# A fused recurrence and two-layer kernel: the first layer cut into seven tiles, one in float32 and six split, instead of two and five

## The chip, the cores and the metric

The kernel runs on one core of a Trainium2 chip. The metric is the device time of one execution in microseconds; the figure that counts is the median of the runs.

## The reference, cut to what matters

For each of 4 batches and 8 heads a state of 48 x 48 is carried over 768 positions; the output of a position is read from the state and from the position's own outer product, then the state is decayed by w and the outer product is added. The result, as 3072 tokens of 384, goes through two layers without any residual: the first is `h = max(x @ w_in, 0)`, then `h * h @ w_out` (384 to 2048 to 384); the second is `(x @ w_a) * (x @ w_b) @ w_out` (384 to 1536 to 384).

```python
for t in range(S):
    cur = einsum('bhd,bhe->bhde', u * k[t], v[t])
    y[t] = einsum('bhd,bhde->bhe', r[t], state + cur)
    state = w[t][..., None] * state + einsum('bhd,bhe->bhde', k[t], v[t])
x = y as (3072, 384)
x = maximum(x @ w_in, 0) ** 2 @ w_out
out = ((x @ w_a) * (x @ w_b)) @ w_out2
```

## The kernel before

**Units.** The recurrence is done in chunks of 128 positions. A unit is one batch and one chunk; there are 24, in the order chunk by chunk, four batches in each (`units`), so that unit i is batch i % 4 of chunk i // 4. A unit goes through `prepare` (two scans and some seven more DVE instructions, a ScalarE pass and eight ScalarE scalings of the identity), `scores` (PE, L238 and L242; two predicated copies on DVE, L246), `mix` (PE, L260, L266, L273; the state update on DVE, L291 and L293) and, for all but the first four, `split_x` (L305 on ScalarE, L306 on DVE), which writes the unit's 128 columns of x as a pair of fp32r numbers, high and low part. `prepare` also issues the loads of the unit two further on (`load_unit`, on SyncE's queue); lkr, the tile of k and r, has two buffers.

**First layer.** It is done in tiles of tokens. In each tile 16 steps f run over the hidden dimension. A step makes hp, 128 hidden rows for all tokens of the tile (9 or 3 matmuls), then t = relu(hp) * hp (ScalarE, then DVE), and two steps later `x2_step` adds the product with w_out to three accumulators. hp has two PSUM buffers. The units of the *next* tile are worked on between the steps: `bursts` puts scores and mix of a unit at given steps (BURSTS: eight steps for four units).

Two kinds of tiles exist. The units 0 to 3 (chunk 0) are done in two float32 tiles of 256 columns (loop `half_n`, L401): three plain float32 matmuls for hp (L417) and three for the accumulators (L410). The units 4 to 23 are done in five tiles of 512 columns (loop over c, L442) in split form: `mm3` makes each product of three fp32r matmuls (L310, L311, L312: high by high, high by low, low by high), and t is split as well (`split_g`: gh on ScalarE, L370, gl on DVE, L371).

**Weights.** The 32 blocks of w_in and w_out come as raw 64-bit data. `decode_w1` loads and decodes them into float32 (two instructions each on ScalarE, L41 and L43, and on DVE, L42 and L44), two blocks in each step of the first float32 tile. `split_w1` makes the fp32r pair of a block (L144 on ScalarE, L145 on DVE): four stand in the last steps of the second float32 tile, the others in the first split tile, two a step. The 36 blocks of the second layer's weights are decoded from the second split tile on (`narrow_load`, `narrow_store`), written to DRAM as float32, and in the last tile of the first layer read back (`load_w2`, L160, three buffers ws) and split (`split_w2`, L167 on ScalarE and L168 on DVE), two in a step.

**Order.** The code above is only a priority order: the scheduler of the framework puts the instructions of each engine in an order of its own, by its model of the times, and moves work forward where buffers allow it. The engines then run strictly in that order.

**Second layer.** Six tiles of 512 tokens in split form: bp and ap (9 matmuls of 512 columns each), their product, its split, and 12 matmuls of 384 columns in `o_step` (L519 to L521).

Of the kernel before, what the change touches and what calls it, by code (L numbers as in the profile page):

```python
# [20 lines left out]
C = 128  # L21
NC = S // C
units = [(b, c) for c in range(NC) for b in range(B)]
NU = len(units)
# [47 lines left out]
def chunked_path(ctx, tc, flags, krT, wT, krn, vn, u, w1, w2, w3, w4, w5, out):  # L72
# [59 lines left out]
    def decode_w1():  # L132
        load_w1(3)
        if raw_q:
            dst, n, raw = raw_q.pop(0)
            f = dst[n] = wp.tile([128, 384], F32, tag="w", name="wf")
            decode(nc, f, raw, near)
            split_q.append((dst, n, f))
# [45 lines left out]
        loaded[i] = w, kr, v, nn  # L184

    xt = {}
    x0 = {}
    unit = {}

# [62 lines left out]
    def mix(i):  # L252

        b, c = units[i]
        st = unit.pop(i)
        A, v, s = st["A"], st["v"], states[b]
        ps = p_at.tile([128, G, C], F32, tag="at", name="py")
        if c > 0:
            for g in range(G):
                pe.matmul(  # L260
                    out=ps[0:GP, g, :], lhsT=s[:, g].rearrange("p j d -> p (j d)")[:, 0:GP],
                    rhs=st["r"][:, g, :], start=(g == 0), stop=False, skip_group_check=True,
                )
        for g in range(G):
            for j in range(2):
                pe.matmul(  # L266
                    out=ps[64 * j:64 * j + D, g, :], lhsT=v[:, 2 * g + j, :], rhs=A[:, j, g, :],
                    start=(c == 0), stop=True, skip_group_check=True,
                )
        if c < NC - 1:  # L270
            pk = p_at.tile([128, G, 2, D], F32, tag="at", name="pk")
            for g in range(G):
                pe.matmul(out=pk[0:GP, g], lhsT=st["kt"][:, g, :], rhs=v[:, 2 * g:2 * g + 2, :], start=True, stop=True)  # L273

        def post():
            if c > 0:
                x = at.tile([128, G, C], F32, tag="x", name="xf", bufs=2)
            else:
                if b % 2 == 0:
                    x0[b // 2] = xp.tile([128, G, 2, C], F32, tag="x", name="x0")  # L280
                x = x0[b // 2][:, :, b % 2, :]
# [14 lines left out]
            return (lambda: split_x(i, x)) if c > 0 else None  # L296
        return post

    def split_x(i, xf):
        b, c = units[i]  # L300
        if c not in xt:
            xt[c] = xp.tile([128, 2, 3, T], F32R, tag="x", name="x")
        o = slice(b * C, (b + 1) * C)
        hi, lo = xt[c][:, 0, :, o], xt[c][:, 1, :, o]
        act.activation(out=hi, in_=xf[:, 0:3], func=AF.Copy)  # L305
        dve.tensor_tensor(out=lo, in0=xf[:, 0:3], in1=hi.bitcast(F32), op=ALU.subtract)  # L306

# [59 lines left out]
    def split_g(t):  # L367
        gh = gp.tile([128, T], F32R, tag="gh", name="gh")
        gl = gp.tile([128, T], F32R, tag="gl", name="gl")
        act.activation(out=gh, in_=t, func=AF.Copy)  # L370
        dve.tensor_tensor(out=gl, in0=t, in1=gh.bitcast(F32), op=ALU.subtract)  # L371
        return gh, gl


    def bursts(units_of, at_steps):

        return {f: (units_of[n // 2], n % 2) for n, f in enumerate(at_steps)}

    def burst(plan, f):
        if f not in plan:  # L380
            return None
        i, second = plan[f]
        return (mix if second else scores)(i)
# [14 lines left out]
            act.dma_start(out=x2d[:, m, tok0:tok0 + n], in_=e)  # L398


    for half_n in range(2):  # L401
        x = x0.pop(half_n)
        N = 2 * C
        acc = [p_acc.tile([128, N], F32, tag="acc", name="acc") for _ in range(3)]
        gg = {}

        def x2_step(f):
            t = gg.pop(f)
            for m in range(3):
                pe.matmul(out=acc[m], lhsT=w_out[f][:, m * 128:(m + 1) * 128], rhs=t, start=f == 0, stop=f == 15)  # L410

        plan = bursts((2, 3), (1, 5, 8, 12)) if half_n == 0 else bursts((4, 5, 6, 7), BURSTS)
        prepare(2 if half_n == 0 else 4)
        for f in range(16):
            hp = p_mm.tile([128, N], F32, tag="mm", name="hp")
            for k in range(3):
                pe.matmul(  # L417
                    out=hp, lhsT=w_in[f][:, k * 128:(k + 1) * 128],
                    rhs=x[:, k].rearrange("p b t -> p (b t)"), start=k == 0, stop=k == 2,
                )  # L420
            post = burst(plan, f)
            t = gg[f] = gp.tile([128, N], F32, tag="gh", name="g")
            act.activation(out=t, in_=hp, func=AF.Relu)
            dve.tensor_tensor(out=t, in0=t, in1=hp, op=ALU.mult)
            if half_n == 0:
                decode_w1()
            if tails:
                tails.pop(0)()
            after(plan, f, post)
            if f >= 2:  # L430
                x2_step(f - 2)
            if half_n == 0:
                decode_w1()
            elif f >= 12:
                split_w1()
        x2_step(14)
        x2_step(15)
        while tails:
            tails.pop(0)()
        store_acc(acc, half_n * N, N)  # L440

    narrow_n = [0]  # L442
    for c in range(1, NC):
        x = xt.pop(c)
        xh, xl = x[:, 0], x[:, 1]
        last = c == NC - 1
        acc = [p_acc.tile([128, T], F32, tag="acc", name="acc") for _ in range(3)]
        gg = {}

        def x2_step(f):  # L450
            gh, gl = gg.pop(f)
            for m in range(3):
                mm3(acc[m], w_out[f], m, gh, gl, f == 0, f == 15)

        plan = {} if last else bursts(range(4 * c + 4, 4 * c + 8), BURSTS)
        if not last:
            prepare(4 * c + 4)
        for f in range(16):
            hp = p_mm.tile([128, T], F32, tag="mm", name="hp")
# [3 lines left out]
            t = gp.tile([128, T], F32, tag="t", name="t", bufs=2)  # L463
            act.activation(out=t, in_=hp, func=AF.Relu)  # L464
            dve.tensor_tensor(out=t, in0=t, in1=hp, op=ALU.mult)  # L465
            gg[f] = split_g(t)
            if c == 1:
                split_w1()
            if tails:
                tails.pop(0)()  # L470
            after(plan, f, post)
            if f >= 2:
                x2_step(f - 2)
            if c == 1:
                split_w1()
            elif (c - 2) * 16 + f >= narrow_n[0] * 1.2:
                narrow_n[0] += 1
                narrow_load()
            if narrow_q and (len(narrow_q) > 1 or not narrow):
                narrow_store()  # L480
            if last:
                if f >= 1:
                    load_w2()
                    load_w2()
                if f >= 3:
                    split_w2()
# [9 lines left out]
        store_acc(acc, c * T, T)  # L496
        if c + 1 == NC - 1:
            while narrow_q:
                narrow_store()

# [8 lines left out]
    for i in range(NC):  # L509
# [13 lines left out]
        for f in range(12):  # L523
# [14 lines left out]
            gg[f] = split_g(bs)  # L538
            if i == 0:
                split_w2()  # L540
            if f >= 2:
# [187 lines left out]
```

## Time and profile before

| what | value |
|---|---|
| runs | 1047.23 us median of 3 (1043.69 to 1050.37) |
| profiled execution, its own time | 1045.72 us |
| span of the profiled execution, first to last instruction | 1044.0 us |
| PE busy | 996.7 us, 95% |
| DVE busy | 535.7 us, 51% |
| ACT busy | 443.2 us, 42% |
| mean granted TensorE clock | 0.990 |

PE is TensorE's matmuls, PEld its weight loads, DVE VectorE, ACT ScalarE, SP SyncE. A busy time is the union of the records of an engine in a stretch. The records of neighbouring matmuls overlap, so what a matmul takes from its engine is read from the distance of two starts, not from its duration. One float32 matmul of 256 columns leaves two records, an fp32r one leaves one. The first 118 us hold the start and the first float32 tile, the stretch up to about 174 us the second; the first split tile runs to about 277 us, the last one from about 518 to 592 us; then comes the second layer.

### The profile page before, as it was taken

How to read it: one execution, taken by the hardware profiler on the slowest of the kernel's cores; microseconds unless marked ns; L12 is line 12 of the kernel's file. 1: busy time of each engine (PE TensorE's matmuls, PEld its weight loads, DVE VectorE, ACT ScalarE, POOL GpSimd, SP SyncE). 2: the span in 40 equal slices, each digit the busy share in tenths (PEclk: the TensorE clock that was granted, in tenths of full speed). 3: DMA queues.
4: the chain of work that ended last, by engine and by line, in shares of the span. 5: the costliest groups of instructions: out<-in, count | busy, mean ns of one | idle time of the engine just before them, and what ended most of it. 6: DMA issues, size and time to landing. Idle time of an engine off the chain costs nothing. (4 is left out here: it accounts for less than half of the span.)

```text
span 1044.0 us, 13596 instructions
## 1 busy us (share of the span) xinstructions
PE 996.7 (95%) x5154; PEld 841.7 (81%) x5154; DVE 535.7 (51%) x890; ACT 443.2 (42%) x912; POOL 67.8 (6%) x60
## 2 busy tenths in 40 slices
PE   3789999998899999999999999999999999999996
PEld 2578888776688888888888888888888888888885
DVE  8999787888887568464355522222222222221221
ACT  5687456676754454354255521312312312212221
POOL 4232001000111001000000000000000000000000
PEclk9999999998899999999999999999999999999999
DMA  9776116766741222111133300100100100100000
GB/s 267 221 251 208 51 52 199 229 222 226 253 139 58 82 70 70 37 58 42 43 116 93 112 1 1 61 1 1 61 1 1 41 1 2 40 1 31 1 1 33
DMA packets 47019, 88.14 MB, mean 84 GB/s; under 512 B 7008, under 2 KB 25568, under 8 KB 46944
## 3 DMA queue, kind: packets, MB, share of 16 engines
q1 hardware_dynamic: 40464, 77.74, 24.0%
q10 hardware_dynamic: 6480, 9.44, 2.5%
q8 instruction: 42, 0.69, 0.3%
q14 instruction: 33, 0.27, 0.1%
HBM read 69.46 MB, written 16.52 MB: 82 GB/s over the span
## 5 line engine op out<-in xcount | busy, mean ns | idle before, releaser
L537 DVE TENSOR_TENSOR t<-ap,t 128x512 f32<-128x512 f32 x72 | 49.8, 692 | 283.9 <-PE ap L312 283.8
L370 ACT ACTIVATE gh<-t 128x512 fp32r<-128x512 f32 x152 | 95.9, 631 | 187.0 <-DVE t L537 132.4
L371 DVE TENSOR_TENSOR gl<-t,gh 128x512 fp32r<-128x512 f32 x152 | 107.5, 707 | 66.8 <-ACT gh L370 66.5
L528 ACT ACTIVATE t<-bp 128x512 f32<-128x512 f32 x72 | 43.0, 597 | 163.0 <-PE bp L312 163.0
L310 PE MATMUL hp<-x,w 128*128 128x512 f32 x240 | 96.4, 402 | 8.1 <-DVE t L465 8.0
L519 PE MATMUL acc<-w,gh 128*128 128x384 f32 x288 | 96.9, 336 | 0.0
L520 PE MATMUL acc<-w,gh 128*128 128x384 f32 x288 | 96.7, 336 | 0.0
L311 PE MATMUL acc<-gl,w 128*128 128x512 f32 x240 | 94.4, 393 | 1.9 <-DVE gl L371 1.8
L521 PE MATMUL acc<-w,gl 128*128 128x384 f32 x288 | 95.1, 337 | 0.0
L312 PE MATMUL hp<-x,w 128*128 128x512 f32 x240 | 95.0, 396 | 0.0
L311 PE MATMUL hp<-x,w 128*128 128x512 f32 x240 | 95.0, 396 | 0.0
L465 DVE TENSOR_TENSOR t<-t,hp 128x512 f32<-128x512 f32 x80 | 54.5, 681 | 77.5 <-ACT t L464 77.5
L312 PE MATMUL acc<-gh,w 128*128 128x512 f32 x240 | 93.9, 391 | 0.0
L310 PE MATMUL acc<-gh,w 128*128 128x512 f32 x240 | 93.6, 408 | 0.0
L312 PE MATMUL bp<-x,w 128*128 128x512 f32 x216 | 85.2, 395 | 0.0
L311 PE MATMUL bp<-x,w 128*128 128x512 f32 x216 | 85.1, 394 | 0.0
L464 ACT ACTIVATE t<-hp 128x512 f32<-128x512 f32 x80 | 47.3, 591 | 88.3 <-PE hp L312 88.2
L312 PE MATMUL ap<-x,w 128*128 128x512 f32 x216 | 84.1, 389 | 0.0
L311 PE MATMUL ap<-x,w 128*128 128x512 f32 x216 | 84.1, 389 | 0.0
L310 PE MATMUL ap<-x,w 128*128 128x512 f32 x216 | 84.0, 389 | 0.0
L310 PE MATMUL bp<-x,w 128*128 128x512 f32 x216 | 84.0, 389 | 0.0
L225 ACT ACTIVATE A<-ident,dd 128x128 f32<-128x128 f32 x192 | 58.7, 391 | 8.7 <-DVE dd L222 8.2
(93 smaller groups left out, 1753.0 us busy)
## 6 DMA issues: line engine op xcount, KB each, us to landing
raw<-in_w SPq DMA_DIRECT2D x68, 384.0 KB, 5.3
lkr<-in_krT SPq DMA_DIRECT2D x24, 448.0 KB, 4.0
nn<-in_krn SPq DMA_DIRECT2D x24, 384.0 KB, 4.1
w2d<-f SPq DMA_DIRECT2D x36, 192.0 KB, 3.6
ws<-w2d SPq DMA_DIRECT2D x36, 192.0 KB, 2.3
lw<-in_wT SPq DMA_DIRECT2D x24, 226.2 KB, 3.1
vn<-in_vn SPq DMA_DIRECT2D x24, 192.0 KB, 2.7
out<-e ACTq DMA_DIRECT2D x24, 192.0 KB, 1.9
```

Of the source, the lines that this page charges most:

```text
L225: act.activation(out=A[:, h % 2, h // 2, :], in_=ident, func=AF.Copy, scale=dd[:, h])
L310: pe.matmul(out=out, lhsT=wt[:, 0, sl], rhs=rhs_hi, start=first, stop=False)
L311: pe.matmul(out=out, lhsT=wt[:, 0, sl], rhs=rhs_lo, start=False, stop=False)
L312: pe.matmul(out=out, lhsT=wt[:, 1, sl], rhs=rhs_hi, start=False, stop=last)
L370: act.activation(out=gh, in_=t, func=AF.Copy)
L371: dve.tensor_tensor(out=gl, in0=t, in1=gh.bitcast(F32), op=ALU.subtract)
L464: act.activation(out=t, in_=hp, func=AF.Relu)
L465: dve.tensor_tensor(out=t, in0=t, in1=hp, op=ALU.mult)
L519: pe.matmul(out=acc[t], lhsT=ph[:, sl], rhs=w_o[f][:, 0, :], start=(f == 0), stop=False)
L520: pe.matmul(out=acc[t], lhsT=ph[:, sl], rhs=w_o[f][:, 1, :], start=False, stop=False)
L521: pe.matmul(out=acc[t], lhsT=pl[:, sl], rhs=w_o[f][:, 0, :], start=False, stop=(f == 11))
L537: dve.tensor_tensor(out=bs, in0=ap, in1=bs, op=ALU.mult)
```

## The change

The tiles of the first layer are cut in another way. A list `tiles` names their units: the first has units 0 and 1, then come five of four units (2 to 5, 6 to 9, ... 18 to 21), and the last has units 22 and 23. Only the first one is float32; the second float32 tile is gone. The last tile is split and has 256 columns. So 16 steps of three and three float32 matmuls of 256 columns go, and 16 steps of nine and nine fp32r matmuls of 256 columns come, at the other end of the layer. The units that are worked on in the float32 tile are now 2 to 5 (before 2 and 3, and 4 to 7 in the second one); the last full tile has only two units to work on. Units 2 and 3 are written in split form now. `split_w1` starts in the last four steps of the only float32 tile. `narrow_load` is spaced by 1.6 steps, where it was 1.2.

```diff
+    tiles = [(0, 1)] + [tuple(range(i, i + 4)) for i in range(2, NU - 2, 4)] + [(NU - 2, NU - 1)]
...
-            if c > 0:
+            if i > 1:
                 x = at.tile([128, G, C], F32, tag="x", name="xf", bufs=2)
...
-            return (lambda: split_x(i, x)) if c > 0 else None
+            return (lambda: split_x(i, x)) if i > 1 else None
...
     def split_x(i, xf):
-        b, c = units[i]
-        if c not in xt:
-            xt[c] = xp.tile([128, 2, 3, T], F32R, tag="x", name="x")
-        o = slice(b * C, (b + 1) * C)
-        hi, lo = xt[c][:, 0, :, o], xt[c][:, 1, :, o]
+        n, o = (i + 2) // 4, (i + 2) % 4
+        if n not in xt:
+            xt[n] = xp.tile([128, 2, 3, T], F32R, tag="x", name="x")
+        o = slice(o * C, (o + 1) * C)
+        hi, lo = xt[n][:, 0, :, o], xt[n][:, 1, :, o]
...
-    for half_n in range(2):
-        x = x0.pop(half_n)
-        N = 2 * C
...
-        plan = bursts((2, 3), (1, 5, 8, 12)) if half_n == 0 else bursts((4, 5, 6, 7), BURSTS)
-        prepare(2 if half_n == 0 else 4)
...
+    plan = bursts(tiles[1], BURSTS)
+    prepare(2)
+    for f in range(16):
+        hp = p_mm.tile([128, N], F32, tag="mm", name="hp")
...
+        decode_w1()
+        if f >= 12:
+            split_w1()
...
-    for c in range(1, NC):
-        x = xt.pop(c)
-        xh, xl = x[:, 0], x[:, 1]
-        last = c == NC - 1
-        acc = [p_acc.tile([128, T], F32, tag="acc", name="acc") for _ in range(3)]
+    for n in range(1, len(tiles)):
+        x = xt.pop(n)
+        N = len(tiles[n]) * C
+        xh, xl = x[:, 0, :, 0:N], x[:, 1, :, 0:N]
+        last = n == len(tiles) - 1
...
-        plan = {} if last else bursts(range(4 * c + 4, 4 * c + 8), BURSTS)
+        plan = {} if last else bursts(tiles[n + 1], BURSTS)
...
-            if c == 1:
+            if n == 1:
                 split_w1()
...
-            elif (c - 2) * 16 + f >= narrow_n[0] * 1.2:
+            elif (n - 2) * 16 + f >= narrow_n[0] * 1.6:
                 narrow_n[0] += 1
                 narrow_load()
```

In the excerpts of the order below the lines of the changed kernel are one higher than before as far as L372 (the float32 steps keep theirs, L410 to L424), and one lower at L464, where t is multiplied by hp.

The first place is DVE where most of the first layer's weights are split. Before, it lies in the second float32 tile; g is the product of a float32 step, w a split weight block, lkr a unit's tile of k and r in `prepare`:

```order
L424 TENSOR_TENSOR g_1087<-g_1087,hp_1065 128x256
L145 TENSOR_TENSOR w_1683<-wf_552,w_1683 128x384
L205 TENSOR_TENSOR lkr_1126<-lkr_1126,fq_1390 112x512
L207 TENSOR_TENSOR lkr_1126<-lkr_1126,fq_1390 112x512
L145 TENSOR_TENSOR w_1695<-wf_604,w_1695 128x384
L209 SCALAR_TENSOR_TENSOR lkr_1126<-lw_1125,lkr_1126 112x512
L424 TENSOR_TENSOR g_1155<-g_1155,hp_1136 128x256
L145 TENSOR_TENSOR w_1733<-wf_618,w_1733 128x384
L145 TENSOR_TENSOR w_1788<-wf_628,w_1788 128x384
```

In the changed kernel it comes after the last g of the only float32 tile, three splits behind it, and the excerpt ends with t_1116, the first product of the first split tile:

```order
L247 COPY_PREDICATED A_1220<-mask_132,ps_1294 128x512
L247 COPY_PREDICATED A_1220<-mask_132,ps_1295 128x512
L201 RECIPROCAL d2_135<-fq_1416 112x4
L206 TENSOR_TENSOR lkr_1084<-lkr_1084,fq_1416 112x512
L214 TENSOR_TENSOR pe2_1424<-fq_1416,half_136 112x8
L145 TENSOR_TENSOR w_1281<-wf_559,w_1281 128x384
L145 TENSOR_TENSOR w_1316<-wf_588,w_1316 128x384
L145 TENSOR_TENSOR w_1332<-wf_602,w_1332 128x384
L145 TENSOR_TENSOR w_1352<-wf_616,w_1352 128x384
L202 SCALAR_TENSOR_TENSOR fq_1416<-lw_1083,d2_135 112x516
L464 TENSOR_TENSOR t_1116<-t_1116,hp_1091 128x512
```

Before, two splits stand between two float32 products; now seven splits, two predicated copies and part of a `prepare` stand between the last float32 product and the first split one.

The second place is DVE in the last tile of the first layer; ws is a block of the second layer's weights read back from DRAM, w its split, t and gl the two products of a step. Before:

```order
L465 TENSOR_TENSOR t_5091<-t_5091,hp_5081 128x512
L168 TENSOR_TENSOR w_5255<-ws_5179,w_5255 128x384
L371 TENSOR_TENSOR gl_5095<-t_5091,gh_5094 128x512
L168 TENSOR_TENSOR w_5258<-ws_5181,w_5258 128x384
L465 TENSOR_TENSOR t_5127<-t_5127,hp_5117 128x512
```

and in the changed kernel:

```order
L464 TENSOR_TENSOR t_5389<-t_5389,hp_5379 128x256
L168 TENSOR_TENSOR w_5588<-ws_5477,w_5588 128x384
L372 TENSOR_TENSOR gl_5393<-t_5389,gh_5392 128x256
L168 TENSOR_TENSOR w_5591<-ws_5479,w_5591 128x384
L464 TENSOR_TENSOR t_5425<-t_5425,hp_5415 128x256
```

The pattern of a step is the same, two splits in each, but the step's own two products have half the columns, as have its 18 matmuls.

## Rows read from the trace of the kernel before

**Rows 1.** The page's first part, busy time of each engine.

```profile
PE 996.7 (95%) x5154; PEld 841.7 (81%) x5154; DVE 535.7 (51%) x890; ACT 443.2 (42%) x912; POOL 67.8 (6%) x60
```

**Rows 2.** Stretches: length, busy PE, PEld, DVE, ACT, POOL; clock, DMA share, GB/s.

```profile
20.00:118.00 98.00, 86.87 (x472) 70.99 (x472) 94.49 (x167) 71.03 (x167) 28.60 (x20) 0.98 0.65 209
118.00:174.00 56.00, 56.00 (x314) 46.71 (x313) 41.03 (x78) 32.73 (x81) 5.44 (x4) 1.00 0.25 78
174.00:339.00 165.00, 154.73 (x862) 124.03 (x861) 136.00 (x229) 105.52 (x227) 17.61 (x14) 0.96 0.61 195
339.00:505.00 166.00, 166.00 (x957) 135.50 (x956) 97.13 (x156) 75.43 (x160) 7.57 (x6) 1.00 0.19 57
505.00:596.00 91.00, 91.00 (x418) 75.03 (x417) 47.12 (x82) 46.45 (x87) 0.00 (x0) 1.00 0.33 99
```

**Rows 3.** PE in order of time, float32 matmuls of 256 columns: start, length.

```profile
125.69 1.46 PE L417 MATMUL hp<-x,wf 128*128 128x256 f32 x6
126.99 1.46 PE L410 MATMUL acc<-g,wf 128*128 128x256 f32 x6
```

**Rows 4.** PE in order of time, other matmuls, in three stretches.

```profile
94.27 0.55 PE L242 MATMUL pt<-ident,lkr 112*128 112x112 f32 x4
94.66 1.47 PE L417 MATMUL hp<-x,wf 128*128 128x256 f32 x6
...
562.80 0.39 PE L310 MATMUL acc<-gh,w 128*128 128x512 f32 x1
...
564.85 0.39 PE L310 MATMUL hp<-x,w 128*128 128x512 f32 x1
...
605.30 0.33 PE L519 MATMUL acc<-w,gh 128*128 128x384 f32 x1
...
606.18 0.34 PE L521 MATMUL acc<-w,gl 128*128 128x384 f32 x1
```

**Rows 5.** Groups of weight loads: count, busy us, mean ns, idle before.

```profile
L519 PEld LDWEIGHTS acc<-w,gh 128*128 128x128 f32 x288 | 54.1, 188 | 2.6
```

**Rows 6.** Groups of DVE instructions from 118 to 174 us.

```profile
L145 DVE TENSOR_TENSOR w<-wf,w 128x384 fp32r<-128x384 f32 x28 | 16.0, 582 | 2.6 <-ACT w L144 2.6
...
L246 DVE COPY_PREDICATED A<-mask,ps 128x512 f32<-128x512 int32 x4 | 2.8, 726 | 0.0
L208 DVE TENSOR_TENSOR lw<-fq 112x512 f32<-112x512 f32 x2 | 2.6, 1308 | 0.0
L196 DVE TENSOR_TENSOR_SCAN fq<-lw,d 112x516 f32<-112x516 f32 x2 | 2.5, 1229 | 0.0
...
L205 DVE TENSOR_TENSOR lkr<-lkr,fq 112x512 f32<-112x512 f32 x2 | 1.4, 692 | 2.1 <-DMA lkr<-in_krT 2.1
...
L213 DVE TENSOR_TENSOR pe<-fq,half 112x8 f32<-112x8 f32 x2 | 0.3, 158 | 0.0
```

**Rows 7.** The page's groups, DVE's products of a split step, whole span.

```profile
L371 DVE TENSOR_TENSOR gl<-t,gh 128x512 fp32r<-128x512 f32 x152 | 107.5, 707 | 66.8 <-ACT gh L370 66.5
...
L465 DVE TENSOR_TENSOR t<-t,hp 128x512 f32<-128x512 f32 x80 | 54.5, 681 | 77.5 <-ACT t L464 77.5
```

**Rows 8.** Waits, whole span: us in total, times, longest.

```profile
DVE lkr L205 <- DMA lkr<-in_krT: 26.2, 18, 2.8
...
PE hp L310 <- DVE t L465: 8.0, 2, 4.6
```

**Rows 9.** One more stretch, columns as in the second group.

```profile
230.00:260.00 30.00, 25.30 (x132) 19.95 (x131) 23.37 (x41) 20.50 (x46) 2.43 (x2) 0.89 0.71 229
```

**Rows 10.** Tile ws from 530 to 595 us: durations in ns, loads' landing.

```profile
L167 ACT ACTIVATE w<-ws x30: 509/516/527, 531.8 to 594.0; 128x384 fp32r<-128x384 f32 x30
L168 DVE TENSOR_TENSOR w<-ws,w x30: 550/551/559, 532.7 to 594.5; 128x384 fp32r<-128x384 f32 x30
...
DMA to landing us min/median/max: 2.1/2.3/3.3
```

**Rows 11.** ScalarE in order of time, early in the last tile.

```profile
530.83 0.63 ACT L363 ACTIVATE x<-x2b 128x512 fp32r<-128x512 f32 x1 [2.88 <-DMA x2b<-x2d]
```

More of the change, by code (lines that the diff above doesn't have):

```diff
@@ L275, in post @@
         def post():
-            if c > 0:
+            if i > 1:
                 x = at.tile([128, G, C], F32, tag="x", name="xf", bufs=2)
             else:
-                if b % 2 == 0:
-                    x0[b // 2] = xp.tile([128, G, 2, C], F32, tag="x", name="x0")
-                x = x0[b // 2][:, :, b % 2, :]
+                if i == 0:
+                    x0[0] = xp.tile([128, G, 2, C], F32, tag="x", name="x0")
+                x = x0[0][:, :, i, :]
             for rows in ((slice(0, GP),) if c > 0 else (slice(0, D), slice(64, GP))):
@@ L365, in split_x2, with split_g @@
         x2[i] = hi, lo
-    def split_g(t):
-        gh = gp.tile([128, T], F32R, tag="gh", name="gh")
-        gl = gp.tile([128, T], F32R, tag="gl", name="gl")
+    def split_g(t, n):
+        gh = gp.tile([128, n], F32R, tag="gh", name="gh")
+        gl = gp.tile([128, n], F32R, tag="gl", name="gl")
         act.activation(out=gh, in_=t, func=AF.Copy)
@@ L375, in bursts @@
     def bursts(units_of, at_steps):
-        return {f: (units_of[n // 2], n % 2) for n, f in enumerate(at_steps)}
+        return {f: (units_of[n // 2], n % 2) for n, f in enumerate(at_steps) if n // 2 < len(units_of)}
     def burst(plan, f):
@@ L398, in store_acc @@
             act.dma_start(out=x2d[:, m, tok0:tok0 + n], in_=e)
-    for half_n in range(2):
-        x = x0.pop(half_n)
-        N = 2 * C
-        acc = [p_acc.tile([128, N], F32, tag="acc", name="acc") for _ in range(3)]
[L405 to L410, printed above, removed]
-        plan = bursts((2, 3), (1, 5, 8, 12)) if half_n == 0 else bursts((4, 5, 6, 7), BURSTS)
-        prepare(2 if half_n == 0 else 4)
[L414 to L440, printed above, removed]
@@ L442, in chunked_path, with x2_step @@
-    narrow_n = [0]
-    for c in range(1, NC):
-        x = xt.pop(c)
-        xh, xl = x[:, 0], x[:, 1]
-        last = c == NC - 1
-        acc = [p_acc.tile([128, T], F32, tag="acc", name="acc") for _ in range(3)]
+    x = x0.pop(0)
+    N = 2 * C
+    acc = [p_acc.tile([128, N], F32, tag="acc", name="acc") for _ in range(3)]
+    gg = {}
+    def x2_step(f):
+        t = gg.pop(f)
+        for m in range(3):
+            pe.matmul(out=acc[m], lhsT=w_out[f][:, m * 128:(m + 1) * 128], rhs=t, start=f == 0, stop=f == 15)
@@ new lines, in chunked_path @@
+    plan = bursts(tiles[1], BURSTS)
+    prepare(2)
+    for f in range(16):
+        hp = p_mm.tile([128, N], F32, tag="mm", name="hp")
+        for k in range(3):
+            pe.matmul(
+                out=hp, lhsT=w_in[f][:, k * 128:(k + 1) * 128],
+                rhs=x[:, k].rearrange("p b t -> p (b t)"), start=k == 0, stop=k == 2,
+            )
+        post = burst(plan, f)
+        t = gg[f] = gp.tile([128, N], F32, tag="gh", name="g")
+        act.activation(out=t, in_=hp, func=AF.Relu)
+        dve.tensor_tensor(out=t, in0=t, in1=hp, op=ALU.mult)
+        decode_w1()
+        if tails:
+            tails.pop(0)()
+        after(plan, f, post)
+        if f >= 2:
+            x2_step(f - 2)
+        decode_w1()
+        if f >= 12:
+            split_w1()
@@ L448, in chunked_path @@
+    x2_step(14)
+    x2_step(15)
+    while tails:
+        tails.pop(0)()
+    store_acc(acc, 0, N)
+    narrow_n = [0]
+    for n in range(1, len(tiles)):
[3 more added lines that the diff above has]
+        last = n == len(tiles) - 1
+        acc = [p_acc.tile([128, N], F32, tag="acc", name="acc") for _ in range(3)]
         gg = {}
@@ L453, in x2_step @@
                 mm3(acc[m], w_out[f], m, gh, gl, f == 0, f == 15)
-        plan = {} if last else bursts(range(4 * c + 4, 4 * c + 8), BURSTS)
+        plan = {} if last else bursts(tiles[n + 1], BURSTS)
         if not last:
-            prepare(4 * c + 4)
+            prepare(tiles[n + 1][0])
         for f in range(16):
-            hp = p_mm.tile([128, T], F32, tag="mm", name="hp")
+            hp = p_mm.tile([128, N], F32, tag="mm", name="hp")
             for k in range(3):
@@ L462, in chunked_path @@
             post = burst(plan, f)
-            t = gp.tile([128, T], F32, tag="t", name="t", bufs=2)
+            t = gp.tile([128, N], F32, tag="t", name="t", bufs=2)
             act.activation(out=t, in_=hp, func=AF.Relu)
             dve.tensor_tensor(out=t, in0=t, in1=hp, op=ALU.mult)
-            gg[f] = split_g(t)
-            if c == 1:
+            gg[f] = split_g(t, N)
+            if n == 1:
                 split_w1()
@@ L473, in chunked_path @@
                 x2_step(f - 2)
-            if c == 1:
+            if n == 1:
                 split_w1()
-            elif (c - 2) * 16 + f >= narrow_n[0] * 1.2:
+            elif (n - 2) * 16 + f >= narrow_n[0] * 1.6:
                 narrow_n[0] += 1
@@ L495, in chunked_path @@
             tails.pop(0)()
-        store_acc(acc, c * T, T)
-        if c + 1 == NC - 1:
+        store_acc(acc, tiles[n][0] * C, N)
+        if n + 1 == len(tiles) - 1:
             while narrow_q:
@@ L537, in chunked_path @@
             dve.tensor_tensor(out=bs, in0=ap, in1=bs, op=ALU.mult)
-            gg[f] = split_g(bs)
+            gg[f] = split_g(bs, T)
             if i == 0:
```

## Prediction

> **What bounds the kernel now.** I read the busy times first, then the stretches, then single rows where stretches left a question. PE is busy for 95% of the span [rows 1], so a change is worth what it takes from or gives to PE, unless another engine makes PE wait. The stretches show where that happens [rows 2]. From 20 to 118 us DVE is busy for 94.5 of 98 us and PE for 86.9: DVE (decoding of weights, `prepare` of the first seven units) sets the pace, and PE fills its time with what is ready. From 118 to 174 us PE is busy throughout and DVE for 41 of 56 us: the second float32 tile lets DVE breathe, and the splits of the first layer's weights are done in that room. From 174 to 339 us both are near their limit: PE is busy for 154.7 of 165 us at a mean granted clock of 0.96, DVE for 136 us. After that PE is busy without a gap to the end of the first layer. The waits name what PE lacks in the tight stretch: twice, 8.0 us in total, the product t of DVE (L465), and DVE itself waited 18 times, up to 2.8 us, for a unit's load lkr [rows 8].
>
> **PE's own work.** Two groups of three float32 matmuls of 256 columns start 126.99 - 125.69 = 1.30 us apart [rows 3]: 0.433 us for one. The dropped tile has 16 x 6 = 96 of them, 41.6 us. The trace has no fp32r matmul of 256 columns. Nine of 512 columns take 564.85 - 562.80 = 2.05 us, 0.228 each, and five of 384 take 0.88 us, 0.176 each [rows 4]; 128 columns are thus worth 0.052 us, and 256 columns come to 0.124. The new tile has 16 x 18 = 288, 35.7 us. PE's work falls by 5.9 us. The attention matmuls of all units stay, as does everything in the second layer.
>
> This supposes that a weight load still hides under a shorter matmul; every fp32r matmul has one of its own, of 128 columns. The lower bound is the line just drawn. The upper one is the load's record, 188 ns on average [rows 5]: 288 x 0.188 = 54.1 us, so that PE's work would grow by 12.5 us. The nearest row speaks for the lower: four transposes, each with a load of 128 columns, start within 94.66 - 94.27 = 0.39 us [rows 4], 0.098 each, so a load can follow the next in less than 0.124. I take 0.124.
>
> The Trainium skill has a rule against this: "TensorE: Matmul & The Clock Gate", section "LDWEIGHTS (loading the stationary operand)", puts a load at its columns divided by 1.2, in ns, and the page's Part 3 on packing says that loads overlap running matmuls only where the row group differs. By both, a load of 128 columns would stand 107 ns beside each matmul, and the tile would cost some 31 us more than I reckon (an estimate from that page). The trace doesn't bear that out: at 512 columns the spacing is 0.228 us, which leaves no room for an unhidden load.
>
> **The start.** In the float32 tile units 2 to 5 are now worked on instead of 2 and 3, so one would fear that the first split tile waits for two more units. But the order before has them in the same DVE stretch already: up to the last g of the only float32 tile DVE has about 200 instructions, of the same kinds as the first 200 before, which fill the stretch to 118 us; PE has then done the float32 tile and units 0 to 6 in the one case, and the first tile, three steps of the second and the same units in the other, within 1 us of the same work by the prices used here. I count nothing; since DVE is full in this stretch [rows 2], where a three per cent change in its order is 3 us, the bounds are -3 and +3.
>
> **The splits lose their room.** What follows is new. Between that g and the sixth t of the first split tile DVE has 62 instructions: 24 splits of 0.582 (14.0 us), 4 scans of 1.23 (4.9), 4 predicated copies of 0.726 (2.9), 2 of L208 at 1.308 (2.6) and 18 others between 0.158 and 0.692 (9.2) [rows 6], 6 products t of 0.681 and 4 gl of 0.707 (6.9) [rows 7], 40.5 us as records. Records overlap their neighbours, so this is the upper end; the union of 167 DVE instructions in the full stretch is 94.5 us, 0.566 each [rows 2], and by that mean the 62 take 35 us. I take 35 to 36. PE has 102 fp32r matmuls of 0.228 (23.3 us), the last 6 float32 ones (2.6) and between two and three units' attention (about 10): 36 us. Before, DVE had 73% to do in the corresponding 56 us; now both need the whole time, as they do before between 174 and 339 us. There PE loses 10.3 us of 165 to waits and 4% to the clock [rows 2], some 10% together. I take 10% of 36 us, 4 us. Bounds: 0, if the order holds as it stands, and 14.5, if each of the four units' loads is waited for by 2.8 us [rows 8] (11.2 us) and the clock falls as it does where PE idles in the stretch from 230 us on, to 0.89 on average over 30 us [rows 9] (3.3 us).
>
> **The narrow stretch.** The 36 decodes of the second layer's weights stand in 19 consecutive steps before (the first split tile and three steps) and in 19 now (from the seventh step of the first split tile on), with four to five units among them in both. The factor 1.6 hardly shows in the order, since the loads are pulled forward as buffers come free. So the loss of 174 to 339 us moves with them and I count 0; the bounds are -10 (all of PE's idle time there goes) and +6.
>
> **The last tile.** It still reads back and splits two blocks in a step, but a step's 18 matmuls take 2.23 us instead of 4.1. DVE has two splits of 0.55 and two half products, ScalarE the same: both fit (DVE 1.1 + about 0.8 = 1.9 us). The loads are tighter: a buffer ws is taken for 2.3 us of landing, 0.52 on ScalarE and 0.55 on DVE [rows 10], about 3.5 us with the hand-overs, and three buffers give two blocks in 2.3 us. In the order, 27 matmuls of the second layer (6.1 us; 8 before) now stand among the tile's steps, which makes a step 2.6 us on average. So the loads just fit. Early in the tile ScalarE waits for x2b, behind the store of the tile before: 2.88 us already before [rows 11], hidden then by steps of 4.1 us. I take 2 us for both. Bounds: 0, and with loads that land in 3.3 us (4.5 us a cycle, 3.0 us a step, 16 x 0.4 = 6.4) and the x2b wait in full, 9.
>
> **Sum.** -5.9 + 0 + 4 + 0 + 2 = about 0 to the nearest microsecond. The profiled execution took 1045.7 us, the median of the runs is 1.5 us higher; I predict 1046 us, that is, no change that a measurement can tell. (About 1% is what one can tell from no change here.)
>
> **Rivals.**
> - *Weight splits and attention starve PE.* The new tight stretch costs its upper bound, 14.5 us instead of 4: -5.9 + 14.5 + 2 = +10.6, 1056 us. It decides as soon as the waits for lkr fall in the 35 us behind the float32 tile. For it: DVE, ScalarE and PE are all full there, and engines run strictly in order. Against it: the loads of weights are over by then, and before 174 us lkr was waited for by only 2.1 us [rows 6]. 17%.
> - *The last tile is bound by reading back weights.* 9 instead of 2: -5.9 + 4 + 9 = +7, 1053 us. For it: three buffers and half the time. Against: the filler. 12%.
> - *The narrow stretch loosens.* The decodes meet other steps and PE's 10.3 us of waits go: -5.9 + 4 + 2 - 10.3 = -10, 1035.5 us. For it: these waits are few and long, so chance decides them. Against: the same density. 13%.
> - *The split tile is not cheaper.* Weight loads bind at 0.188: 54.1 - 41.6 = +12.5, with the other terms +18, 1064 us. Against it stand the transposes. The rule of the skill's page on TensorE that I set against the rows above is this rival in a harder form. 6%.
>
> **How the numbers follow.** My forecast has 52%, from about 1038 to 1054 us on its own bounds. Slower by more than 1% (over 1057) comes from half of the first rival, the last and the edge of the forecast: 17%. Faster by more than 1% (under 1037) comes from most of the third and the other edge: 14%. The rest is 69%. The range 1035 to 1058 leaves out the split tile's rival and the far ends.
>
> **What would show it.** In the changed profile: fp32r matmuls of 256 columns 0.124 us apart (wrong above 0.14); the store of the float32 tile's accumulators near 120 us as before; PE's idle time between 120 and 160 us near 4 us; the two long waits for t again, between 160 and 260 us; the last tile's steps 2.3 to 2.7 us apart and no wait of ScalarE for ws over 1 us. The forecast is wrong if PE's idle time behind the float32 tile is over 10 us, if the clock stays below 0.9 there, or if the waits of the tight stretch are gone.

## The result, and the profile after

The changed kernel takes 1029.84 us (median of 4 runs, 1028.38 to 1031.38) against 1047.08 us of the kernel before beside it; the ratio is 0.9846, 95% interval 0.9825 to 0.9867: 17 us faster by the medians, 16 by the ratio. The forecast was 1046 us with a range from 1035 us: the time lies below it. The profiled execution has a span of 1028.1 us, 15.9 us less than before.

The page's busy times of the changed kernel (line numbers have moved by one, up or down):

```profile
PE 984.1 (96%) x5250; PEld 834.4 (81%) x5250; DVE 540.5 (53%) x908; ACT 448.3 (44%) x930; POOL 72.7 (7%) x60
```

Its stretches, columns as in [rows 2]:

```profile
20.00:118.00 98.00, 86.78 (x514) 71.40 (x515) 97.13 (x173) 77.03 (x187) 32.70 (x21) 1.00 0.69 219
118.00:174.00 56.00, 54.78 (x306) 43.76 (x305) 56.00 (x99) 40.42 (x88) 9.15 (x6) 1.00 0.45 143
174.00:339.00 165.00, 159.09 (x890) 126.70 (x889) 131.22 (x222) 104.42 (x221) 17.52 (x14) 1.00 0.55 176
339.00:505.00 166.00, 166.00 (x938) 135.38 (x937) 91.48 (x147) 72.31 (x150) 5.28 (x4) 1.00 0.18 52
505.00:596.00 91.00, 91.00 (x544) 81.56 (x543) 48.23 (x96) 46.12 (x99) 0.00 (x0) 1.00 0.32 94
```

PE's waits from 118 to 596 us, and DVE's for lkr from 118 to 300 us:

```profile
PE hp L311 <- DVE t L464: 2.7, 3, 1.2
PE ps L239 <- ACT xf L284: 2.6, 1, 2.6
PE acc L312 <- DVE gl L372: 1.8, 2, 1.6
...
DVE lkr L206 <- DMA lkr<-in_krT: 3.5, 2, 2.5
```

Beside [rows 1, 2, 8]: PE is busy for 12.6 us less and idle for 3.3 us less. From 20 to 118 us PE's busy time is the same (its clock is 1.00 where it was 0.98). From 118 to 174 us DVE has not one idle moment, and PE still misses only 1.2 us. The surprise is the stretch from 174 us on: the two waits for t that made 8.0 us are now 2.7 us in three pieces (all behind 118 us), and the granted clock is 1.00 where it was 0.96. From 174 to 345 us, first the kernel before, then the changed one:

```profile
174.00:345.00 171.00, 160.73 (x907) 129.15 (x906) 139.39 (x235) 109.57 (x238) 17.61 (x14) 0.96 0.60 191
174.00:345.00 171.00, 165.09 (x936) 131.82 (x935) 134.86 (x227) 106.97 (x227) 17.52 (x14) 1.00 0.54 171
```

Most of that lies in 70 us; the kernel before:

```profile
230.00:300.00 70.00, 61.90 (x319) 48.59 (x318) 58.91 (x100) 47.37 (x102) 8.24 (x6) 0.90 0.68 219
```

The changed kernel, the same stretch:

```profile
230.00:300.00 70.00, 65.29 (x369) 52.04 (x370) 55.58 (x96) 41.15 (x88) 8.47 (x6) 1.00 0.52 162
```

A clock of 0.90 is a mean between the two levels, 1.2 and 2.4 GHz. The two long waits, 4.6 and 3.4 us, end at 238.84 and 265.13 us, inside this stretch, and toward the end of each the clock falls to the lower level (the kernel before; ahead of each fall, then in it):

```profile
234.00:237.20 3.20, 0.27 (x2) 0.00 (x0) 3.20 (x7) 3.03 (x7) 0.00 (x0) 1.00 0.37 85
237.30:244.00 6.70, 5.03 (x11) 3.55 (x12) 6.70 (x9) 3.13 (x6) 2.43 (x2) 0.50 0.81 275
261.00:264.50 3.50, 0.73 (x9) 0.52 (x8) 3.50 (x7) 2.54 (x6) 0.00 (x0) 1.00 0.57 167
264.60:271.30 6.70, 6.17 (x14) 4.25 (x14) 6.70 (x10) 3.94 (x7) 2.65 (x2) 0.50 0.76 264
```

So PE first stands, and when its work arrives it is busy for 11.2 us at half the clock: 5.6 us lost. The changed kernel has no wait over 2.6 us behind 118 us and no fall.

The new matmuls, PE in order of time in the last tile:

```profile
549.67 0.28 PE L311 MATMUL hp<-x,w 128*128 128x256 f32 x1
549.79 0.28 PE L312 MATMUL hp<-x,w 128*128 128x256 f32 x1
549.91 0.28 PE L313 MATMUL hp<-x,w 128*128 128x256 f32 x1
550.03 0.28 PE L311 MATMUL hp<-x,w 128*128 128x256 f32 x1
```

They start 0.120 us apart: 288 take 34.6 us, where the dropped tile had 41.6 us. So the difference of 15.9 us is, to about 1 us: 7.0 of PE's own work, 3.2 of its waits behind 118 us (10.3 before, 7.1 now), 5.6 of clock from 174 to 345 us.

### The profile page after: what moved, and what is told of

It reads as the page before. It is cut to its first block, busy times and chain, and to the rows that moved or that the text cites. A ratio compares the mean times of both kernels' runs of the same rounds, so it can differ in the third digit from the quotient of the medians.

```text
span 1028.1 us, 13834 instructions
## 1 busy us (share of the span) xinstructions
PE 984.1 (96%) x5250; PEld 834.4 (81%) x5250; DVE 540.5 (53%) x908; ACT 448.3 (44%) x930; POOL 72.7 (7%) x60
## 5 line engine op out<-in xcount | busy, mean ns | idle before, releaser
L371 ACT ACTIVATE gh<-t 128x512 fp32r<-128x512 f32 (+1 forms) x168 | 102.4, 609 | 185.3 <-DVE t L536 127.0
L372 DVE TENSOR_TENSOR gl<-t,gh 128x512 fp32r<-128x512 f32 (+1 forms) x168 | 112.1, 667 | 74.7 <-ACT gh L371 74.4
L311 PE MATMUL hp<-x,w 128*128 128x512 f32 (+1 forms) x288 | 109.3, 379 | 2.7 <-DVE t L464 2.7
L312 PE MATMUL acc<-gl,w 128*128 128x512 f32 (+1 forms) x288 | 108.2, 376 | 1.9 <-DVE gl L372 1.8
L313 PE MATMUL acc<-gh,w 128*128 128x512 f32 (+1 forms) x288 | 107.5, 374 | 0.0
L312 PE MATMUL hp<-x,w 128*128 128x512 f32 (+1 forms) x288 | 107.2, 372 | 0.0
L313 PE MATMUL hp<-x,w 128*128 128x512 f32 (+1 forms) x288 | 107.1, 372 | 0.0
L311 PE MATMUL acc<-gh,w 128*128 128x512 f32 (+1 forms) x288 | 102.6, 383 | 0.0
L464 DVE TENSOR_TENSOR t<-t,hp 128x512 f32<-128x512 f32 (+1 forms) x96 | 61.0, 635 | 74.0 <-ACT t L463 74.0
L463 ACT ACTIVATE t<-hp 128x512 f32<-128x512 f32 (+1 forms) x96 | 53.3, 555 | 83.2 <-PE hp L313 81.3
L311 PEld LDWEIGHTS hp<-x,w 128*128 128x128 f32 x288 | 54.2, 188 | 14.4 <-DVE t L464 4.3
```

Of the source, the lines that this page charges most:

```text
L311: pe.matmul(out=out, lhsT=wt[:, 0, sl], rhs=rhs_hi, start=first, stop=False)
L312: pe.matmul(out=out, lhsT=wt[:, 0, sl], rhs=rhs_lo, start=False, stop=False)
L313: pe.matmul(out=out, lhsT=wt[:, 1, sl], rhs=rhs_hi, start=False, stop=last)
```

## Experiments

Each time stands beside runs of the kernel before on the same chip, 1045.5 to 1047.2 us. One measure recurs: the time between ScalarE's Relu of two steps of the first layer (steps counted through, 16 to a tile), from the 29th to the 97th in kernels cut like the one before and from the 17th to the 97th in those cut like the changed one, less the same time without the pass over the second layer's weights (e3, e4). I call it **the cost of the decodes**. In ScalarE's order of time its two ends are, for the kernel before:

```profile
153.27 0.38 ACT L423 ACTIVATE g<-hp 128x256 f32<-128x256 f32 x1 [0.77 <-PE hp L417]
...
521.81 0.60 ACT L464 ACTIVATE t<-hp 128x512 f32<-128x512 f32 x1 [4.39 <-PE hp L312]
```

And for e3:

```profile
157.10 0.38 ACT L423 ACTIVATE g<-hp 128x256 f32<-128x256 f32 x1 [0.77 <-PE hp L417]
...
506.80 0.60 ACT L464 ACTIVATE t<-hp 128x512 f32<-128x512 f32 x1 [4.39 <-PE hp L312]
```

368.5 - 349.7 = 18.8 us before, and by the same reading 413.8 - 404.5 = 9.3 us after. In these steps PE has no wait in e3 and e4, and the clock is 1.00 in both. Below are all kernels (PE's waits in the steps named; the longest; the mean clock from 174 to 345 us; ScalarE's waits for raw to land in those steps). Each figure is from one execution; those of e13, e14 and e18 were the quickest of their runs, 3 to 4 us under the median, and those of e4 and e5 were the slowest, 4 and 6 us over it. The clock is that from 174 to 345 us even where the steps reach further.

```
                     cost  PE's waits  longest  clock  waits for raw
before               18.8     10.1       4.6     0.96      21.8
e5 stores on POOL    23.7     14.1       4.5     0.95      29.2
e7 lkr on POOL       16.1     11.1       3.3     0.99      24.0
e9 splits doubled    18.7     12.2       4.4     0.97      20.5
e11 units on POOL    25.9     15.8       5.2     0.93      15.5
e13 no stores        11.9      5.3       4.2     0.98      23.9
e14 no computing     17.2     11.9       4.7     0.96       -
e17 spread           21.3     11.6       3.9     0.99      68.3
after                 9.3      7.1       2.6     1.00      12.5
e1 factor             9.0      5.0       1.6     0.99      12.4
e6 stores on POOL    13.6      8.7       2.7     0.98      22.6
e8 two products      10.1      5.9       2.2     0.98      13.0
e10 splits doubled   10.2      5.3       1.4     0.99      19.5
e12 units on POOL    26.6     18.5       6.5     0.96      12.9
e15 no stores        11.4      4.8       1.6     0.99      21.0
e16 no computing     11.0      6.6       4.5     0.98       -
e18 spread            8.9      7.2       1.7     1.00      86.3
```

### Which part of the change: e1, e2

```diff
-            elif (n - 2) * 16 + f >= narrow_n[0] * 1.6:
+            elif (n - 2) * 16 + f >= narrow_n[0] * 1.2:
```

> The changed kernel with the old factor 1.2 in the condition for loading the second layer's weights; nothing else differs. Theory A (the cut itself does it: in the new order of steps and units, units find their loads landed, PE has no long wait in the stretch of the second layer's decodes and its clock doesn't fall): the factor decides nothing, 1030 us, within 3. Theory B (the looser factor 1.6 thins the decodes out and so frees DVE): 1040 us or more, with PE waits of over 2.6 us back between 118 and 300 us.

1030.1 us: the factor does nothing. As the prediction said, loads run ahead of their place as buffers come free; in the trace the order of every engine and of SP's queue is that of the changed kernel, row for row. So e1 is a second execution of the same order, and the table shows by how much two of them differ: 5.0 against 7.1 us of waits, a clock of 0.99 against 1.00, and nearly the same cost, 9.0 against 9.3 us.

```diff
-    tiles = [(0, 1)] + [tuple(range(i, i + 4)) for i in range(2, NU - 2, 4)] + [(NU - 2, NU - 1)]
+    tiles = [(0, 1), (2, 3)] + [tuple(range(i, i + 4)) for i in range(4, NU, 4)]
...
-        n, o = (i + 2) // 4, (i + 2) % 4
+        n, o = (i // 4 + 1, i % 4) if i > 3 else (1, i - 2)
```

> The changed kernel cut 2, 2, 4, 4, 4, 4, 4: the split tile of 256 columns stands second, where the second float32 tile stood, and units are worked on beside the same tiles as before. It takes the conversion to the split form alone, without the shifted cut. Theory A (the shifted cut decides): only PE's cheaper matmuls are gained, 7.0 us (96 of 0.433 against 288 of 0.120), less what DVE lacks for the weights' splits beside a tile that is now shorter: 1040 to 1046 us, with long PE waits (over 2.6 us) or a granted clock under 0.95 between 118 and 300 us. Theory C (any removal of the second float32 tile gives it, wherever the half tile stands): 1030 us, within 3.

1038.82 us, ratio 0.9936 (0.9914 to 0.9959): about 7 us. That is the size of PE's own gain, but not that gain alone. The clock from 174 to 345 us is 0.99 here, one fall of 3.4 us that costs at most 1.7 us where the kernel before loses 5.6; so some 4 of the 7 us are clock. And the tile of 256 columns, standing in the tight stretch, is hardly cheaper than the float32 tile. Its 288 matmuls, the distances of their starts added up without PE's waits, take 40.5 us (41.6 for the dropped tile, 34.5 by the same reading in the changed kernel), mostly because 39 of them have the next start 0.15 to 0.25 us behind (one in the changed kernel):

```profile
123.31 0.39 PE L311 MATMUL acc<-gh,w 128*128 128x256 f32 x1
123.53 0.28 PE L311 MATMUL hp<-x,w 128*128 128x256 f32 x1
123.65 0.28 PE L312 MATMUL hp<-x,w 128*128 128x256 f32 x1
```

PE's waits from 118 to 345 us stay at 10.7 us, though none is over 2.8 us. The other 9 us of the change come only with the shifted cut, and some 6 of them are these matmuls, undisturbed in the last tile. Theory C falls; the time lies a little under the 1040 to 1046 us of theory A.

### What the decodes cost in either cut: e3, e4

```diff
-    narrow = list(enumerate(order2))
+    narrow = []
...
-            sync.dma_start(out=raw, in_=w2d[n])
+            sync.dma_start(out=raw, in_=vn[f * 128:(f + 1) * 128])
```

> The kernel before without the first pass over the second layer's weights: their loading, decoding and storing is left out, and the later pass reads rows of another input in their place. Theory A: the whole loss of the kernel before in 174 to 339 us hangs on these decodes, PE's 10.3 us of waits there and the fallen clock (0.96 over 165 us, 6.6 us): 1047 - 17 = 1030 us or down to 1027. Theory D (the loss comes from attention and the units' loads, decodes or not): 1043 us or more, and waits for lkr stay over 10 us in sum.

> The changed kernel with the same part left out. Theory A: here the decodes cost little, since PE waits only 7 us and the clock stays at 1.00: 1030 - 2 to 7 = 1023 to 1028 us, and the difference to the kernel before with the same part left out falls from 17 us to about PE's own 7. Theory D: the difference stays at about 17 us.

1029.99 us for the one: PE has no wait behind 118 us, though DVE still waits 8.2 us for lkr between 170 and 300 us. Theory D falls: waits of that length hold nobody up where DVE has no decodes to do. The other gave 1027.64 us, only 2.2 us under the changed kernel and 2.4 under e3, where theory A had 7, with a slower start (its 17th step comes at 134.3 us instead of 121.4, PE being idle for 18.0 instead of 11.2 us from 20 to 118 us, at a clock of 0.93 there); hence the cost by steps. It is 18.8 and 9.3 us: what the new cut gains beside PE's own work lies in the steps of the decodes.

### Late loads on SP's queue: e5 to e7

```diff
-        sync.dma_start(out=w2d[n], in_=decode(...
+        pool.dma_start(out=w2d[n], in_=decode(...
```

> The kernel before, with the stores of the second layer's decoded weights (L154) issued from POOL's queue instead of SP's. On SP these stores wait for DVE's decodes, 43.7 us in sum between 174 and 300 us, and the units' loads of lkr stand behind them. Theory E (late lkr loads hold DVE for 2 to 3 us each, the decodes pile up behind them, t is late, PE waits and its clock falls): the waits for lkr between 174 and 300 us fall from 11.1 us to under 4, PE's waits there from 10.3 us to under 5, the clock stays over 0.97, and the time falls by 6 to 13 us, to 1034 to 1041 us. Theory F (DVE simply has too much to do beside the decodes; the late loads are a symptom): lkr's waits may go, PE's waits of 8 us or more and the fallen clock stay, 1044 us or more.

> The same edit in the changed kernel. Theory E: its units already find their loads landed until 219 us, there are 5.9 us of PE waits left between 174 and 345 us, so at most some of these go: 1026 to 1030 us. Theory F: no change, 1030 us.

```diff
-        sync.dma_start(out=kr, in_=krT[b, c])
+        pool.dma_start(out=kr, in_=krT[b, c])
```

> The kernel before, with the units' loads of lkr (L181) issued from POOL's queue instead of SP's, where no store stands ahead of them. This moves the order at the start too, which may cost or give some us there. Theory E: waits for lkr between 174 and 300 us under 4 us, PE's waits there under 5 us, 1034 to 1041 us. Theory F: 1044 us or more.

1049.62, 1036.22 and 1045.01 us: two are slower than what they edit (e6 slower than either theory had it), the third the same (1.0000, 0.9983 to 1.0018). In e5 DVE now waits for the stores to give back f's buffers, 8.9 us between 170 and 295 us. In e7 DVE waits for lkr not once between 170 and 300 us, and PE waits as long as before. From 118 to 345 us its waits have other names:

```profile
PE acc L311 <- DVE gl L371: 4.5, 3, 3.3
PE hp L310 <- DVE t L465: 2.8, 2, 2.0
PE ps L238 <- ACT xf L283: 2.3, 1, 2.3
```

Theory E falls. In e7 the clock stays at 0.99 from 174 us on, and the cost is 2.7 us lower with 1.0 us more of waits: this speaks for a price of the clock of its own, of some 4 us.

### The last tile: e8

```diff
+                mm3(hp, w_in[f], k, xh[:, k, :], xl[:, k, :], k == 0, k == 2, mid=not last)
...
+        if mid:
             pe.matmul(out=out, lhsT=wt[:, 0, sl], rhs=rhs_lo, start=False, stop=False)
```

(The same argument stands at the call for acc. What is left out of the last tile is the high half of the weights by the low half of the activations; the expectation has the halves the wrong way round, which changes nothing in the count.)

> The changed kernel with the last tile making two of its three products (the high half of the activations by the low half of the weights is left out), which takes 96 matmuls of 256 columns out of it. If PE sets the pace of the last tile: 96 x 0.120 = 11.5 us less, 1018 to 1019 us. If reading back the weights sets it, or is about to: less than half of that, 1024 us or more, with ScalarE's waits for ws over 1.1 us.

1021.61 us, 8.2 us less: between the two. PE's waits in the last tile come to 1.4 us, so PE sets most of its pace: from the tile's first step to the end the profiled execution takes 483.6 us where the changed kernel takes 492.9, 9.3 us of the 11.5. It comes to that step 1.7 us later; its clock was 0.95 from 230 to 300 us.

### DVE's load: e9 to e12

```diff
-            dve.tensor_tensor(out=t[:, 1, :], in0=f, in1=t[:, 0, :].bitcast(F32), op=ALU.subtract)
+            for _ in range(2): dve.tensor_tensor(out=t[:, 1, :], in0=f, in1=t[:, 0, :].bitcast(F32), op=ALU.subtract)
```

> The kernel before, with DVE's half of each weight split (L145) done twice, 32 instructions of 0.58 us more, 18.6 us of DVE, some 16 of them behind 118 us. Theory G (until the second layer's decodes are done DVE is what bounds; the kernel before leaves DVE idle for 15 of the 56 us between 118 and 174 us, because its splits follow the second float32 tile, and pays for this idle time later, in the decodes; the changed kernel has DVE busy for 56 of 56 us there): the additional work fits in the idle time, 1046 to 1051 us. Theory H (the order of DVE's queue against its waits happens to be better in the changed kernel; DVE's load as such doesn't bind): the doubled work costs both kernels the same within 4 us.

> The same edit in the changed kernel. Theory G: DVE has no idle time there, so the 18.6 us are paid for the most part, 10 to 17 us: 1040 to 1047 us, with a first decode some 10 us or more later than 152 us. Theory H: the same cost as in the kernel before, within 4 us.

1047.06 and 1031.11 us: 32 more instructions, 18.6 us as records (DVE's busy time rises by 11.0 us in either kernel), cost 1 to 2 us in the kernel before and, by the medians or by the ratios (0.9891 against 0.9846), 1 to 5 in the changed one. In e10 DVE is full for 110.7 of 112 us, and PE lacks 3.8 us:

```profile
118.00:174.00 56.00, 53.89 (x311) 41.72 (x309) 56.00 (x102) 34.55 (x79) 7.87 (x6) 1.00 0.23 68
174.00:230.00 56.00, 54.29 (x277) 41.16 (x277) 54.71 (x97) 38.94 (x78) 6.22 (x4) 1.00 0.65 217
```

Theory G falls. A full DVE alone does not starve PE.

```diff
-        dve.tensor_tensor(out=r, in0=r, in1=f[:, :, 0:C], op=ALU.mult)
+        (pool if i > 1 else dve).tensor_tensor(out=r, in0=r, in1=f[:, :, 0:C], op=ALU.mult)
...
-        dve.tensor_tensor(out=lo, in0=xf[:, 0:3], in1=hi.bitcast(F32), op=ALU.subtract)
+        pool.tensor_tensor(out=lo, in0=xf[:, 0:3], in1=hi.bitcast(F32), op=ALU.subtract)
```

> The kernel before, with two of DVE's instructions of each unit from the third on moved to POOL: the product r by f (L205, 0.69 us) and the low half of x (L306, 0.57 us; in the float32 tiles' units there is none). This takes some 7 us off DVE in the stretch of the decodes and some 3 us at the start; on POOL they take about 1.35 to 1.8 us each (estimated from its 1.35 us for 128x384), beside 2.7 us that it already has in a unit. Theory G: a gain of 5 to 11 us, 1036 to 1041 us. Theory H: within 3 us of 1046.

> The same edit in the changed kernel. Theory G: DVE binds here too, from the start to 262 us, so 4 to 10 us are gained, 1020 to 1026 us, with no PE wait over 2 us left between 174 and 345 us. Theory H: within 3 us of 1030.

1053.17 and 1051.37 us: less work on DVE made both slower, the changed kernel by 21.5 us. Neither theory had that. POOL's order is strict too, and r now stands on it behind a load and ahead of the low half of x. POOL's waits in e12, 20 to 300 us:

```profile
POOL lkr L206 <- DMA lkr<-in_krT: 71.8, 6, 23.3
POOL x L307 <- ACT x L306: 53.1, 10, 14.0
```

### Computing or traffic, dense or spread: e13 to e18

In e13 and e15:

```diff
-        sync.dma_start(out=w2d[n], in_=decode(nc, wr.tile([128, 384], F32, tag="ws", name="f"), raw, near))
+        decode(nc, wr.tile([128, 384], F32, tag="ws", name="f"), raw, near)
```

And, in e14 and e16, with the same line taken out:

```diff
+        sync.dma_start(out=w2d[n], in_=raw[:, 0:384])
```

(The later pass reads rows of vn in all four.)

> The kernel before, whose decodes of the second layer's weights are computed but not stored; the later pass reads rows of another input in their place. Theory S (the stores hold SP's queue while they wait for a decode, loads behind them come late, and DVE and ScalarE wait for those): most of the 16 us goes, 1030 to 1036 us, and ScalarE's waits for raw fall from 21.8 us to under 8. Theory K (the computing itself, four operations of a block in the strict queues of DVE and ScalarE, delays t): at most a third goes, 1041 us or more.

> The kernel before, whose blocks of the second layer are loaded and half of each is stored as loaded, without decoding; the later pass reads rows of another input. The traffic is the same, and DVE and ScalarE have 144 operations less. Theory K: 1030 to 1034 us. Theory T (the traffic delays the units' loads): 1041 us or more, with lkr waits of over 11 us between 170 and 295 us. Theory S: the stores wait only for a load, not for a decode, so 1030 to 1036 us too; e13 tells it from K.

> The changed kernel with the stores left out as in e13. Theory S: SP's waits for decodes cost little here, 1026 to 1030 us. Theory K: 1029 to 1031 us.

> The changed kernel with the computing left out as in e14. Theory K: PE's 5.9 us of waits between 174 and 345 us go, 1023 to 1026 us. Theories S and T: 1027 to 1030 us.

1043.6, 1047.4, 1033.43 and 1038.97 us; the last two are longer than any theory had them. Without computing the kernel before is as slow as with it, and the changed one slower, partly at the start (its 17th step comes 7.3 us later). DVE has time to spare in e14 (34.0 of 56 us from 174 to 230 us), stands before late loads, and PE waits for t behind it (170 to 300 us for DVE, 118 to 345 us for PE):

```profile
DVE lkr L205 <- DMA lkr<-in_krT: 26.2, 5, 8.7
...
PE hp L310 <- DVE t L465: 11.9, 3, 4.7
```

So theories F and K fall: the pass's transfers are enough to make the whole cost, 17.2 us in this cut and 11.0 in the other. That they make it by the same waits when the computing is there isn't shown: in e14 lkr is waited for by 26.2 us, in the kernel before by 11.1. Dropping the stores takes a third of it before (by the medians 3.6 us) and nothing after; S falls too.

```diff
+            raw = wp.tile([128, 2 * 3 * 128], I32, tag="w", name="raw")
+            act.activation(out=raw.bitcast(F32)[:, 0:1], in_=t[:, 0:1], func=AF.Copy)
+            sync.dma_start(out=raw, in_=src[f])
```

(In the function that loads a block; t is that of the step.)

> The kernel before, with each load of the second layer's weights tied to the step at which the code asks for it, by a ScalarE copy of one column of that step's t into the buffer ahead of the load (36 small instructions more). The 36 decodes then stand in some 43 steps, 1.2 apart, and not in 20. Theory T (density: loads, stores and units' loads crowd SP's queue and the transfers, DVE's strict queue holds t behind late ones): most of the 17 us goes, 1029 to 1036 us, with the clock at 1.00 and PE's waits between 174 and 345 us under 4 us. Theory K (each block costs, wherever it stands): 1044 us or more.

> The same edit in the changed kernel; the decodes then stand in 57 steps, 1.6 apart. Theory T: most of the 10 us goes, 1019 to 1025 us, PE's waits between 118 and 345 us under 3 us. Theory K: 1028 us or more.

1047.73 and 1033.1 us. The spreading worked: up to the 53rd step e17 runs like e3 (275.1 against 276.8 us), then it loses the same again where the blocks now stand, with a clock of 0.97 from 345 to 505 us. A load tied to its step lands late, and ScalarE waits for raw for 68 and 86 us. So the edit brings waits of its own, and e17 speaks against theory T's density without excluding it; e18 has the longest waits for raw at no more cost than the changed kernel.

No experiment beat the changed kernel as it stands; e4 and e8, which are quicker, leave work out.

## Why the prediction was wrong

- **PE's own work**, -5.9: right. The spacing is 0.120 us where 0.124 was reckoned, so -7.0. It holds where the tile now stands; in e2, in the tight stretch, the same tile gained about 1 us. So the rival of a split tile that isn't cheaper falls for this cut alone. The rule of the Trainium skill's page "TensorE: Matmul & The Clock Gate" (section "LDWEIGHTS (loading the stationary operand)" and Part 3) does not hold in this tile: 107 ns of load beside each matmul do not fit into 0.120 us.
- **The start**, 0: right; PE is idle for 11.2 us from 20 to 118 us, 11.1 before.
- **The splits lose their room**, +4: DVE is full as foreseen, but PE lacks 1.2 us. That two full engines lose 10% was the wrong premise; e10 shows it with DVE fuller still.
- **The narrow stretch**, "So the loss of 174 to 339 us moves with them and I count 0": this step failed. PE's waits from 174 to 345 us fell from 10.3 to 5.9 us, and the clock went from 0.96 to 1.00: 4.4 + 5.6 = 10.0 us. That is the third rival, held at 13% against "the same density". The term's own lower bound, -10, was just reached, but it stood for PE's waits alone: the prediction left the clock that fell with them out of this term, although both stood in the same row. The rival's time would come out at 1035.5 - 5.6 = 1030 us with the clock; that it meets the measured one is luck, since the waits fell by 4.4 us and not by 10.3, and the +4 and +2 in it did not come.
- **The last tile**, +2: nothing. PE is busy for 91 of 91 us. ScalarE does wait for ws, up to 2.0 us where at most 1 was promised, and the steps, by ScalarE's Relu, lie 1.5 to 4.2 us apart, 2.7 on average, where 2.3 to 2.7 was promised; PE has other work meanwhile (ScalarE's waits, 530 to 590 us):

```profile
ACT w L167 <- DMA ws<-w2d: 6.2, 10, 2.0
```

By what was measured the sum is -7.0 + 0 + 1.2 - 10.0 + 0 = -15.8, against -15.9.

**What stays open.** Why the decodes cost 9.3 us in the new cut and 18.8 in the old is narrowed, not settled. Not decisive are lkr's place on SP's queue (e7), the stores' queue (e5, e6) and DVE's load (e9, e10); the factor (e1) changes no order, and how densely the blocks stand (e17, e18) is tried only with waits added. Nor does it look like the luck of one order: doubled splits move some 90 to 330 rows on each of PE, DVE and ScalarE, and each cut keeps its level (18.7 in e9, 10.2 in e10). The table shows PE's waits and the clock moving with the cost (of 18.8 us they name 15.7, of 9.3 they name 7.1; the rest has no name), but the transfers' lateness does not follow it: e18 has the longest waits for raw at the cost of the changed kernel. How the units' loads interleave with the blocks in each cut was not tried by itself; no run has a third buffer of lkr.

## What to carry to other kernels

Price a stall with the clock that falls with it: here 10 us of waits came with 6 us of clock, and a gain of 4 us in the waits came with all 6 of the clock. Ask where a new tile will stand, too: the same matmuls took 34.5 us in a quiet stretch and 40.5 in a full one. Where several engines work in strict order beside late transfers, "it only moves" is a guess: leave the pass out once, and take the whole of what it costs as the range of that term. Less work on the fullest engine can lose time, and more can be nearly free, when it is an order of waits and not a load that binds.

## What the runs showed of the hardware

- A product of 112x512 takes 1.703 us on POOL in e12 (its groups from 20 to 300 us), 0.692 on DVE [rows 6]:

```profile
L206 POOL TENSOR_TENSOR lkr<-lkr,fq 112x512 f32<-112x512 f32 x13 | 22.1, 1703 | 95.7 <-DMA lkr<-in_krT 71.8 <-PE ps L239 12.8 <-DVE t L292 5.5
```

- The clock fell further where waits were more and longer: e6 with 8.7 us of waits, none over 2.7, kept 0.98, and e11 with 15.8 us, the longest 5.2, fell to 0.93. Sum and longest wait grow together in these kernels, so which of them counts isn't shown, and the line isn't clean: e7, with 11.1 us and 3.3 the longest, kept 0.99, and e1, with 5.0 us and 1.6 the longest, had a fall that the changed kernel, with 7.1 and 2.6 us in the same order, had not.
